# Channel attention and two feed-forward layers on one core: the float64 weights' low word added as an integer on VectorE

## The chip, the cores and the metric

One core of a Trainium2 chip. The time is device microseconds (us) of one launch; loading inputs and storing the output are in it. Engines: TensorE (PE, with its weight loads as PEld), VectorE (DVE), ScalarE (ACT), GpSimd (POOL) and SyncE (SP), which issues all DMAs here.

## What is computed

q, k and v are [6016, 256], float32. The attention runs over channels, and its output goes through two layers with 2048 hidden columns.

```python
qn = q / (np.linalg.norm(q, axis=1, keepdims=True) + 1e-06)
kn = k / (np.linalg.norm(k, axis=1, keepdims=True) + 1e-06)
s = kn.transpose(0, 2, 1) @ qn / tau
a = softmax(s)                           # 256 x 256
x = v @ a                                # 6016 x 256
h = x @ moe_w_in;  g = h - np.tanh(h);  x = g @ moe_w_out
h = x @ moe2_w_in; g = np.where(h > 0, h, np.exp(np.minimum(h, 0)) - 1)
return g @ moe2_w_out
```

The four weights (256 x 2048 or 2048 x 256) are float64: each is two 32-bit words, low and high.

## The kernel before

Every float32 operand of a product is held as two float32r parts, hi and lo, and a product is hi·hi + hi·lo + lo·hi: three matmuls.

**Attention, up to about 56 us.** q and k come in chunks; their squared norms and the 256 x 256 scores are summed, then the softmax is taken and transposed. The first conversions of weights already run there.

**Folding.** The softmax's matrix is multiplied into the first layer's w_in in place (`fold_attention`, in eight parts: "aw", twelve matmuls of 128x256 each, L406), so that v itself enters the first layer. `evac_fold` writes hi on ScalarE (L428) and lo on VectorE (L434).

**The two layers.** Tokens go in 13 blocks of up to 464, columns of the hidden layer in eight pairs of 128. A unit is (layer, block, pair) and is one step of the last loop. In each step TensorE's order is: the unit's h (`emit_h`, twelve matmuls of 128x464, L406), a fold where one is due, and o of the unit two steps before (`emit_out`, twelve matmuls, L574). h lies in one of two PSUM buffers. It is free once VectorE has read it: in layer 0 by g = h - tanh(h) (L494), in layer 1 by L517. A fold from the third on uses one of these two buffers as well. All instructions stand in an order written out by hand; each engine takes its own in that order.

The first ten steps alternate between blocks 0 and 1 of layer 0, six more finish them, eight do block 2, and then units of layer 1 and layer 0 come in turn.

**The conversion of the weights** (`class Converter`) is what the change touches. A unit of it is 512 elements on each partition (24 early units) or 256 (16 late ones), and it goes through stages one step apart, put between the instructions of `emit_act`:

- `load`: the two words by DMA, into one of 4 (late: 3) buffers;
- `first`, ScalarE: the high word's square (L104, "sq") and the low word scaled (L105, "low");
- `second`, VectorE, four instructions that `fill(0)` to `fill(3)` place in the step: flushed (L121), which zeroes what float32 can't hold; shifted (L127) and joined (L133), which build float32's bits of the value cut to 20 bits of mantissa ("cut"); and power (L139), which leaves its power of two in "hz";
- `third_scalar`, ScalarE, in the next step: hi, rounded by its type (L159), from "cut";
- `third_pool`, GpSimd, in the next step: low · power (L167), cut - hi (L168), and their sum, lo (L169).

VectorE's order in a step of blocks 0 to 2 is flushed, L494, L434 where a part was folded, shifted, joined, lo of g (L522), power. ScalarE's is tanh (L493), L428 where a part was folded, hi of the unit before, sq and low of the next, hi of g (L505). L522 waits for L505. From block 3 on, and in layer 1, VectorE rounds g's hi itself (L503, L521). "hz" and "cut" have two buffers each, "sq" two (late: one), "low" four (late: three).

Once the early units are through, their memory is given to the second layer's w_out, and the late units' loads begin. One core does all of it.

Of the kernel before, what the change touches and what calls it, by code (L numbers as in the profile page):

```python
# [8 lines left out]
F32 = mybir.dt.float32  # L9
F32R = mybir.dt.float32r  # L10
U32 = mybir.dt.uint32
AF = mybir.ActivationFunctionType
# [4 lines left out]
P = 128  # L17
#: The high word of 2^-126 as a float64, read as a float32: smaller weights are float32 zeros.
TINY_HIGH = 2.0**-15 * 1.125
# [3 lines left out]
def kernel(  # L23
# [11 lines left out]
):  # L35
    """q, k: [N, C]; vT: [C, N]; the weights: float64 words as [.., .., 2] (low, high); outT: [C, N].

    A float32 operand of a product is held as two parts of 12 significant bits, hi + lo, both
    float32r, so that hi*hi + hi*lo + lo*hi is float32's product to its last bit.
    """  # L40
    nc = tc.nc
# [19 lines left out]

# [1 line left out]
    # A unit is (layer, which, first column or row of d_ff, their number): 2 words of d_ff x C  # L63
    # for each of them on a partition. It goes through its stages one tick apart, so that no
    # engine waits for another within a tick.

    class Converter:
# [29 lines left out]
        def first(self):  # L97
            """ScalarE: the high word's square and the low word's value below 2^-20."""
            if self.at[1] == self.at[0]:
                return  # L100
            s = self.st[self.at[1]]
            s["sq"] = self.tmp.tile([P, self.n], F32, tag="sq", name="sq", bufs=self.nsq)
            s["low"] = self.tmp.tile([P, self.n], F32, tag="low", name="low", bufs=self.nlow)
            nc.scalar.activation(out=s["sq"], in_=s["raw"][:, :, 1].bitcast(F32), func=AF.Square)  # L104
            nc.scalar.activation(out=s["low"], in_=s["raw"][:, :, 0], func=AF.Copy, scale=2.0**-52)  # L105
            self.at[1] += 1

        def second(self):
            """VectorE: float32's bits of the value cut to 20 of the mantissa, and of its power of 2."""
            if self.begun == self.at[1]:  # L110
                return []
            s = self.st[self.begun]
            self.begun += 1
            hz = self.tmp.tile([P, self.n], F32, tag="hz", name="hz")
            cut = self.tmp.tile([P, self.n], U32, tag="cut", name="cut")
            s["pow"], s["cut"] = hz, cut.bitcast(F32)
            high = hz.bitcast(U32)

            def flushed():
                # Zero where the float64 is below float32's normal range.  # L120
                nc.vector.scalar_tensor_tensor(  # L121
                    out=hz, in0=s["sq"], scalar=TINY_HIGH**2, in1=s["raw"][:, :, 1].bitcast(F32),
                    op0=ALU.is_ge, op1=ALU.mult,
                )

            def shifted():
                nc.vector.tensor_scalar(  # L127
                    out=cut, in0=high, scalar1=3, scalar2=0x3FFFFFF8,
                    op0=ALU.logical_shift_left, op1=ALU.bitwise_and,
                )  # L130

            def joined():
                nc.vector.scalar_tensor_tensor(  # L133
                    out=cut, in0=high, scalar=0xC0000000, in1=cut,
                    op0=ALU.bitwise_and, op1=ALU.bitwise_or,
                )

            def power():
                nc.vector.tensor_scalar(  # L139
                    out=high, in0=cut, scalar1=0xFF800000, scalar2=None, op0=ALU.bitwise_and  # L140
                )
                self.at[2] += 1

            return [flushed, shifted, joined, power]

# [6 lines left out]
        def third_scalar(self):  # L152
            """ScalarE: hi, rounded by its type."""
            if self.at[3] == self.at[2]:
# [6 lines left out]
        def third_pool(self):  # L161
            """GpSimd: lo = (cut - hi) + low * power of 2."""
            if self.at[3] == self.at[2]:
                return
            s = self.st.pop(self.at[3])
            low, cut = self.shape(s["low"]), self.shape(s["cut"])
            nc.gpsimd.tensor_tensor(out=low, in0=low, in1=self.shape(s["pow"]), op=ALU.mult)  # L167
            nc.gpsimd.tensor_tensor(out=cut, in0=cut, in1=s["hi"].bitcast(F32), op=ALU.subtract)  # L168
            nc.gpsimd.tensor_tensor(out=s["lo"], in0=cut, in1=low, op=ALU.add)  # L169
            self.at[3] += 1  # L170

    NU = KC * 2 * P
    # w_in is wanted a step ahead of its phase's h, w_out two steps after it.
    SIDE = NP - 3
# [11 lines left out]
    aT_pool = right.enter_context(tc.tile_pool(name="aT", bufs=1, side="right"))  # L186
    # The scores' transpose: for each half of k's channels, q's on the partitions.
    aT_hi = [aT_pool.tile([P, KC, P], F32R, name=f"aT_hi{m}") for m in range(KC)]
    aT_lo = [aT_pool.tile([P, KC, P], F32R, name=f"aT_lo{m}") for m in range(KC)]
    rsum = aT_pool.tile([P, KC], F32, name="rsum")  # L190

# [1 line left out]
    v_of = {}  # L193
# [20 lines left out]
    def attention():  # L214
        with ExitStack() as init:
# [8 lines left out]
            nc.vector.memset(tiny, 1e-36)  # L224
            # The table for the squares and the root is fetched while the first loads are on their way.
            nc.scalar.activation(out=root[:, 0:1], in_=tiny, func=AF.Sqrt)
# [11 lines left out]
            chunks = [(j, min(J, JT - j)) for j in range(0, JT, J)]  # L238
            # Every other chunk's product goes in parts: PE would be behind the loads.
            in_parts = [i % 2 == 1 and i < len(chunks) - 2 for i in range(len(chunks))]  # L240
# [18 lines left out]
            def keep_warm(n):  # L259
                """PE's clock falls when it has nothing to do."""  # L260
                for _ in range(n):
# [48 lines left out]
            for part_of in early.second():  # L310
                part_of()
            # One column of squared norms for each half of q's and of k's channels.
            for t in range(2):
# [22 lines left out]
            keep_warm(3)  # L336
            # 1 / |q| along the free axis, the same on every partition.
            rq = ps_q.tile([P, KC, 512], F32, tag="sq", name="rq", bufs=2)[:, 0, :C]
# [10 lines left out]
            sm = one.tile([P, KC], F32, name="sm")  # L349
            # a: the negative of the scores. Of the softmax, the division by the sum comes with  # L350
            # the product with w_in.
            nc.vector.tensor_scalar_mul(a[:, 0, :], S[0], rk[:, 0:1])
# [32 lines left out]
    with tc.manual_schedule():  # L385
# [16 lines left out]
        def product(out, terms):  # L402
            """out = the sum over terms of lhsT.T @ rhs, each of which is (hi, lo); w_lo comes last."""
            pairs = [(w[0], x) for w, xs in terms for x in xs] + [(w[1], xs[0]) for w, xs in terms]
# [3 lines left out]
        def fold_attention(p):  # L408
            """w_in of the first layer, in place: softmax(..) @ w_in, for v in x's place."""
            fs = slice(2 * P * p, 2 * P * (p + 1))  # L410
# [11 lines left out]
        def evac_fold(p, ps):  # L422
            """With the softmax's division; the parts of it for the two engines."""
            fs = slice(2 * P * p, 2 * P * (p + 1))
# [37 lines left out]
        def emit_act(layer, b, p, h, ticks, fold):  # L462
# [10 lines left out]
            def between():  # L473
                """ScalarE's and GpSimd's part of the conversion."""
                if ticks == 1:
# [5 lines left out]
            if ticks == 2:  # L481
                thirds()
            # VectorE's, each step of which waits for the one before, goes between the others.
            seconds = [conv.second() for _ in range(ticks)]
# [21 lines left out]
            else:  # L506
                # exp(m) - 1 = tanh(m / 2) * (exp(m) + 1), m = min(h, 0): no cancellation near 0.
                e = (late_pool[0] if late_pool else spool_e).tile([P, 2, width], F32, tag="e", name="e")[:, :, :n]
# [17 lines left out]
        def emit_last_act(b, p, h):  # L526
            """The last unit's, one tile of d_ff after the other and on more engines: nothing hides it."""
            _, n = blocks[b]
# [34 lines left out]
        def emit_out(layer, b, p, g):  # L563
# [4 lines left out]
            hi, lo = g  # L568
            # g's lower part comes last.
            for w, x in ((wout_hi, hi), (wout_lo, hi), (wout_hi, lo)):  # L570
# [31 lines left out]
        def interleaved(first, second, lead):  # L602
            """The units of two phases in turn; the second starts `lead` units later."""
            first = [(*first, p) for p in range(NP)]
# [8 lines left out]

        # A phase starts once the output of the one that it reads is on its way.
        order = [(0, b, p) for p in range(SIDE) for b in range(2)]
# [93 lines left out]
```

## Time and profile before

| | |
|---|---|
| time, median of 3 runs | 1149.56 us (1149.43 to 1152.14) |
| span of the profiled execution (its first to its last instruction; the page has no other time of it) | 1147.9 us |
| PE busy | 1116.2 us, 97%, 5360 instructions |
| PEld busy | 991.2 us, 86% |
| DVE busy | 879.0 us, 77%, 957 instructions |
| ACT busy | 555.5 us, 48% |
| POOL busy | 178.3 us, 16%, 137 instructions |
| mean granted TensorE clock | 0.996 |

The page cuts the span into 40 equal slices (28.7 us each); a digit is the busy share in tenths:

```profile
PE   8889998999999999999999999999999999999998
DVE  6999998899866767766677777676776667678776
POOL 5577676355100000000000000000000000000000
```

In the rows below, times are us from the span's start. A busy time of pipelined instructions overlaps the next one's a little; where an argument needs what an instruction costs its engine, it goes from start to start.

### The profile page before, as it was taken

Reading aid. Unit: us, or ns where it says so; the run is one execution under the profiler, and the core shown is the slowest. Engines: PE = TensorE matmul, PEld = TensorE weight load, DVE = VectorE, ACT = ScalarE, POOL = GpSimd, SP = SyncE. Lnnn points to the kernel's source line nnn. Section 1 sums busy time; section 2 is a strip of 40 time slices with the busy share of each in tenths; the row PEclk is TensorE's granted clock in tenths of the full one; section 3 lists DMA queues with packets and bytes.
Section 4 is the critical chain, followed back from the end, with each engine's and each line's share of the span. In section 5 each row is a group of like instructions: output and inputs, shape, how many; then the busy total and the mean of one; then the engine's idle time right before and its main releaser. Section 6 shows DMA issues by size and latency. Waiting matters only on the chain.

```text
span 1147.9 us, 13713 instructions
## 1 busy us (share of the span) xinstructions
PE 1116.2 (97%) x5360; PEld 991.2 (86%) x5360; DVE 879.0 (77%) x957; ACT 555.5 (48%) x662; POOL 178.3 (16%) x137
## 2 busy tenths in 40 slices
PE   8889998999999999999999999999999999999998
PEld 7778887787888888888888888888888889998897
DVE  6999998899866767766677777676776667678776
ACT  7766664664444443444444334434334444445664
POOL 5577676355100000000000000000000000000000
PEclk9999998999999999999999999999999999999999
DMA  9632220220100100100001001001001000000000
GB/s 349 225 109 77 90 90 1 74 67 24 34 1 1 34 1 1 34 1 29 5 1 34 1 1 34 1 1 34 1 1 33 1 12 5 1 17 1 1 34 17
DMA packets 23040, 42.30 MB, mean 37 GB/s; under 512 B 1984, under 2 KB 8896, under 8 KB 22976
## 3 DMA queue, kind: packets, MB, share of 16 engines
q1 hardware_dynamic: 22976, 41.43, 10.8%
q8 instruction: 42, 0.69, 0.2%
q14 instruction: 22, 0.18, 0.0%
HBM read 35.26 MB, written 6.16 MB: 36 GB/s over the span
## 4 chain that ended last, share of the span: by engine, by line
PE 82%; DVE 7%; issue 7%; ACT 1%; POOL 1%; DMA 1%; SPq 0%; DVEq 0%; ACTq 0%
PE h L406 40%; PE o L574 39%; PE S L249 3%; DVE hz L121 1%; DVE cut L127 1%; DVE hz L139 1%; DVE g L517 1%; DVE cut L133 1%; DVE g L494 1%; DMA qk<-in_k_dram 1%; POOL cut L168 0%; POOL win_lo L169 0%; PE aw L406 0%; DVE glo L522 0%; DVE win_lo L434 0%
## 5 line engine op out<-in xcount | busy, mean ns | idle before, releaser
L513 DVE SCALAR_TENSOR_TENSOR g<-e,g 128x928 f32<-128x928 f32 (+1 forms) x103 | 118.9, 1155 | 194.3 <-ACT e L511 194.3
L522 DVE TENSOR_TENSOR glo<-g,ghi 128x928 fp32r<-128x928 f32 (+1 forms) x207 | 242.9, 1173 | 22.4 <-ACT ghi L505 2.7
L509 ACT ACTIVATE e<-h 128x928 f32<-128x928 f32 (+1 forms) x103 | 97.3, 945 | 312.8 <-PE h L406 312.8
L574 PE MATMUL o<-ghi,wout_lo 128*128 128x464 f32 (+1 forms) x832 | 208.7, 372 | 1.6 <-POOL wout_lo L169 1.6
L574 PE MATMUL o<-ghi,wout_hi 128*128 128x464 f32 (+1 forms) x832 | 209.2, 373 | 0.4 <-DVE xlo L591 0.3
L574 PE MATMUL o<-glo,wout_hi 128*128 128x464 f32 (+1 forms) x832 | 208.7, 372 | 0.0
L493 ACT ACTIVATE g<-h 128x928 f32<-128x928 f32 (+1 forms) x104 | 98.0, 942 | 157.6 <-PE h L406 157.6
L574 PEld LDWEIGHTS o<-ghi,wout_lo 128*128 128x128 f32 x832 | 156.1, 188 | 20.6 <-POOL wout_lo L169 2.4
L574 PEld LDWEIGHTS o<-glo,wout_hi 128*128 128x128 f32 x832 | 156.0, 188 | 19.0 <-DVE glo L522 0.2
L574 PEld LDWEIGHTS o<-ghi,wout_hi 128*128 128x128 f32 x832 | 156.4, 189 | 18.5 <-PE h L406 0.7
L406 PE MATMUL h<-vhi,win_hi 128*128 128x464 f32 (+1 forms) x416 | 156.2, 375 | 9.3 <-DVE g L494 8.6
L406 PE MATMUL h<-xhi,win_hi 128*128 128x464 f32 (+1 forms) x414 | 154.6, 374 | 5.6 <-DVE g L517 4.4
L406 PE MATMUL h<-vlo,win_hi 128*128 128x464 f32 (+1 forms) x416 | 155.9, 375 | 0.0
L406 PE MATMUL h<-xlo,win_hi 128*128 128x464 f32 (+1 forms) x414 | 153.5, 371 | 0.0
L517 DVE SCALAR_TENSOR_TENSOR g<-h,g 128x928 f32<-128x928 f32 (+1 forms) x103 | 115.5, 1122 | 10.0
L406 PE MATMUL h<-vhi,win_lo 128*128 128x464 f32 (+1 forms) x416 | 121.5, 373 | 0.3 <-DVE win_lo L434 0.3
L406 PE MATMUL h<-xhi,win_lo 128*128 128x464 f32 (+1 forms) x414 | 119.9, 370 | 0.0
L494 DVE TENSOR_TENSOR g<-h,g 128x928 f32<-128x928 f32 (+1 forms) x104 | 115.8, 1114 | 0.7 <-ACT g L493 0.7
L510 ACT ACTIVATE g<-e 128x928 f32<-128x928 f32 (+1 forms) x103 | 101.0, 981 | 3.2
L511 ACT ACTIVATE e<-e 128x928 f32<-128x928 f32 (+1 forms) x103 | 100.8, 978 | 3.3
L406 PEld LDWEIGHTS h<-vhi,win_hi 128*128 128x128 f32 x416 | 78.5, 189 | 22.3 <-DVE g L494 7.4
L406 PEld LDWEIGHTS h<-xhi,win_hi 128*128 128x128 f32 x414 | 77.7, 188 | 17.4 <-DVE g L517 7.2
(113 smaller groups left out, 1149.2 us busy)
## 6 DMA issues: line engine op xcount, KB each, us to landing
qk<-in_q_dram SPq DMA_DIRECT2D x23, 256.0 KB, 5.1
qk<-in_k_dram SPq DMA_DIRECT2D x23, 256.0 KB, 5.2
vraw<-in_vT_dram SPq DMA_DIRECT2D x12, 464.0 KB, 4.4
out_dram<-osb SPq DMA_DIRECT2D x12, 464.0 KB, 2.9
raw0in<-in_moe_w_in_dram SPq DMA_DIRECT2D x8, 512.0 KB, 3.8
raw0out<-in_moe_w_out_dram SPq DMA_DIRECT2D x8, 512.0 KB, 3.7
raw1in<-in_moe_w_in_dram SPq DMA_DIRECT2D x8, 512.0 KB, 3.8
raw1out<-in_moe_w_out_dram SPq DMA_DIRECT2D x16, 256.0 KB, 2.6
```

Source lines behind the costliest of these rows:

```text
L121: nc.vector.scalar_tensor_tensor(out=hz, in0=s["sq"], scalar=TINY_HIGH**2, in1=s["raw"][:, :, 1].bitcast(F32), op0=ALU.is_ge, op1=ALU.mult,)
L249: nc.tensor.matmul(out=S[m], lhsT=kk[:, 1, j, m * P : (m + 1) * P], rhs=qq[:, 0, j, :], start=(count[m] == 1), stop=(count[m] == total),)
L406: nc.tensor.matmul(out=out, lhsT=w, rhs=x, start=(i == 0), stop=(i == len(pairs) - 1))
L493: nc.scalar.activation(out=g, in_=h, func=AF.Tanh)
L494: nc.vector.tensor_tensor(out=g, in0=h, in1=g, op=ALU.subtract)
L509: nc.scalar.activation(out=e, in_=h, func=AF.Relu, scale=-1.0)
L510: nc.scalar.activation(out=g, in_=e, func=AF.Tanh, scale=-0.5)
L511: nc.scalar.activation(out=e, in_=e, func=AF.Exp, scale=-1.0)
L513: nc.vector.scalar_tensor_tensor(out=g, in0=e, scalar=1.0, in1=g, op0=ALU.add, op1=ALU.mult)
L517: nc.vector.scalar_tensor_tensor(out=g, in0=h, scalar=0.0, in1=g, op0=ALU.max, op1=ALU.add)
L522: nc.vector.tensor_tensor(out=lo, in0=g, in1=hi.bitcast(F32), op=ALU.subtract)
L574: nc.tensor.matmul(out=o[:, c, :n], lhsT=w[layer][:, f, c * P : (c + 1) * P], rhs=x[:, i], start=(f == 0 and w is wout_hi and x is hi), st ...
```

## The change

The low word is scaled by 2^-29 instead of 2^-52 and written as uint32, so that it becomes an integer of three bits, rounded. VectorE's fourth instruction is now the add of this integer to the bits of "cut", where it was the power of two's mask. GpSimd's part is one subtraction, cut - hi, into lo. Comments and docstrings are taken out as well; line numbers stay.

```diff
-            s["low"] = self.tmp.tile([P, self.n], F32, tag="low", name="low", bufs=self.nlow)
+            s["low"] = self.tmp.tile([P, self.n], U32, tag="low", name="low", bufs=self.nlow)
             nc.scalar.activation(out=s["sq"], in_=s["raw"][:, :, 1].bitcast(F32), func=AF.Square)
-            nc.scalar.activation(out=s["low"], in_=s["raw"][:, :, 0], func=AF.Copy, scale=2.0**-52)
+            nc.scalar.activation(out=s["low"], in_=s["raw"][:, :, 0], func=AF.Copy, scale=2.0**-29)
...
-            s["pow"], s["cut"] = hz, cut.bitcast(F32)
+            s["cut"] = cut.bitcast(F32)
...
-            def power():
-                nc.vector.tensor_scalar(
-                    out=high, in0=cut, scalar1=0xFF800000, scalar2=None, op0=ALU.bitwise_and
-                )
+            def rounded():
+
+                nc.vector.tensor_tensor(out=cut, in0=cut, in1=s["low"], op=ALU.add)
                 self.at[2] += 1
 
-            return [flushed, shifted, joined, power]
+            return [flushed, shifted, joined, rounded]
...
             s = self.st.pop(self.at[3])
-            low, cut = self.shape(s["low"]), self.shape(s["cut"])
-            nc.gpsimd.tensor_tensor(out=low, in0=low, in1=self.shape(s["pow"]), op=ALU.mult)
-            nc.gpsimd.tensor_tensor(out=cut, in0=cut, in1=s["hi"].bitcast(F32), op=ALU.subtract)
-            nc.gpsimd.tensor_tensor(out=s["lo"], in0=cut, in1=low, op=ALU.add)
+            nc.gpsimd.tensor_tensor(
+                out=s["lo"], in0=self.shape(s["cut"]), in1=s["hi"].bitcast(F32), op=ALU.subtract
+            )
             self.at[3] += 1
```

## Rows read from the trace of the kernel before

**Rows 1.** Stretches: length, busy us of each engine (instructions), clock, DMA share, GB/s.

```profile
56.57:87.50 30.93, 26.13 (x121) 22.01 (x122) 30.69 (x37) 20.59 (x33) 22.11 (x15) 0.94 0.32 101
87.50:138.12 50.62, 48.15 (x254) 42.85 (x253) 50.34 (x60) 32.57 (x51) 35.77 (x25) 1.00 0.28 84
138.12:205.54 67.42, 59.47 (x265) 50.72 (x263) 60.74 (x62) 36.49 (x52) 45.12 (x30) 0.95 0.19 61
205.54:298.50 92.96, 88.19 (x409) 76.18 (x410) 88.39 (x124) 52.38 (x84) 43.51 (x48) 1.00 0.13 40
```

**Rows 2.** The chain that ended last: start, us, what.

```profile
122.81 1.42 PE aw L406 x12
124.23 2.52 PE o L574 x12
126.74 2.53 PE h L406 x12
```

**Rows 3.** TensorE's waits, 56 to 299 us: us in total, times, longest.

```profile
PE h L406 <- DVE g L494: 9.7, 9, 3.9
PE h L406 <- DVE g L517: 4.4, 7, 1.9
PE aw L406 <- DVE g L494: 3.4, 1, 3.4
PE o L574 <- POOL wout_lo L169: 1.6, 2, 0.9
```

**Rows 4.** VectorE's timeline, two steps around 100 us: start, us, instruction.

```profile
93.68 1.11 DVE L494 TENSOR_TENSOR g<-h,g 128x928 f32<-128x928 f32 x1
94.71 0.86 DVE L434 SCALAR_TENSOR_TENSOR win_lo<-aw,rsum,win_hi 128x256 fp32r<-128x256 f32 x2
...
99.42 0.68 DVE L121 SCALAR_TENSOR_TENSOR hz<-sq,raw0in 128x512 f32<-128x512 f32 x1
100.02 1.11 DVE L494 TENSOR_TENSOR g<-h,g 128x928 f32<-128x928 f32 x1
101.06 0.48 DVE L127 TENSOR_SCALAR cut<-hz 128x512 uint32<-128x512 uint32 x1
101.57 1.68 DVE L133 SCALAR_TENSOR_TENSOR cut<-hz,cut 128x512 uint32<-128x512 uint32 x1
103.17 2.21 DVE L522 TENSOR_TENSOR glo<-g,ghi 128x928 fp32r<-128x928 f32 x1
105.30 0.41 DVE L139 TENSOR_SCALAR hz<-cut 128x512 uint32<-128x512 uint32 x1
...
106.24 1.11 DVE L494 TENSOR_TENSOR g<-h,g 128x928 f32<-128x928 f32 x1
```

**Rows 5.** GpSimd's timeline in the same step; the bracket is its idle time before.

```profile
99.58 1.67 POOL L167 TENSOR_TENSOR low<-low,hz 128x512 f32<-128x512 f32 x1 [2.00 <-DVE hz L139]
101.21 1.48 POOL L168 TENSOR_TENSOR cut<-cut,wout_hi 128x512 f32<-128x512 f32 x1
102.77 1.62 POOL L169 TENSOR_TENSOR wout_lo<-cut,low 128x512 fp32r<-128x512 f32 x1
```

**Rows 6.** VectorE's timeline in the attention.

```profile
40.58 0.69 DVE L299 TENSOR_TENSOR acc<-acc 128x512 f32<-128x512 f32 x1
```

**Rows 7.** ScalarE's timeline, the next step.

```profile
104.23 0.84 ACT L428 ACTIVATE win_hi<-aw,rsum 128x256 fp32r<-128x256 f32 x2 [0.47 <-PE aw L406]
104.96 0.63 ACT L159 ACTIVATE win_hi<-cut 128x512 fp32r<-128x512 f32 x1
105.48 0.68 ACT L104 ACTIVATE sq<-raw0out 128x512 f32<-128x512 f32 x1
...
107.44 0.98 ACT L505 ACTIVATE ghi<-g 128x928 fp32r<-128x928 f32 x1 [0.72 <-DVE g L494]
```

**Rows 8.** VectorE's groups, 205 to 292 us: busy us, mean ns, idle before.

```profile
L513 DVE SCALAR_TENSOR_TENSOR g<-e,g 128x928 f32<-128x928 f32 x8 | 12.2, 1527 | 1.0 <-ACT e L511 1.0
L133 DVE SCALAR_TENSOR_TENSOR cut<-hz,cut 128x256 uint32<-128x256 uint32 x16 | 10.6, 662 | 0.3
```

## The prediction

> **What bounds the kernel now.** I read the page's busy row and its forty slices first: TensorE is busy 97% of the span, so only the stretches where it is not can be won. Behind about 299 us its slices are full until the last; there every cut on VectorE or GpSimd is hidden. The conversion runs from 40 to 294 us, and the loss lies there, from the first h at 56.57 us on.
>
> How much it is follows from counting. One group of twelve matmuls (an h or an o) takes 2.525 us when nothing holds it, one fold (aw) 1.42 [rows 2]. The count of matmuls in each stretch is that of its groups: A, 56.57 to 87.50, holds 5 h, 3 o and 2 folds (23.0 us of work in 30.93: 7.9 lost); B, to 138.12, 8 h, 8 o, 5 folds (47.5 in 50.62: 3.1 lost); C, to 205.54, 11 h and 11 o (55.6 in 67.42: 11.9 lost); D, to 298.50, 17 h and 17 o (85.9 in 92.96: 7.1 lost) [rows 1]. Together 30.0 us: idle time, the refilling after each stop, and a granted clock that averages 0.94 and 0.95 in A and C, where TensorE had stood for its longest waits, 3.4 and 3.9 us [rows 1, 3].
>
> What it waits for is nearly always VectorE's subtraction that frees an h buffer (L494, L517), twice GpSimd's wout_lo [rows 3]. VectorE's line shows why: two steps of the loop, from one L494 to the next, take 6.34 and 6.22 us without a gap, while TensorE needs 6.47 with a fold and 5.05 without, 11.5 for the two [rows 2, 4]. VectorE is the bound in these stretches, and it is slower than its own work. Start to start, L494 takes 1.04 and the subtraction L522 of the same size 2.13; L121 takes 0.60 and L133, with as many elements and two inputs too, 1.60 [rows 4]. The long ones stand beside GpSimd: L168 runs from 101.21 to 102.69 and L133, begun at 101.57, ends 0.56 later; L169 ends at 104.39 and L522 1.0 later [rows 4, 5]. They do their work only once GpSimd's operation is over. L494, which reads one operand from PSUM, runs at full pace beside L167.
>
> The Trainium skill's page "SBUF — State Buffer", section "Who interferes with whom", says that VectorE and GpSimd share a port pair as an exclusive lock: an instruction of VectorE with two SBUF inputs, or in a two-port mode, waits for all of a GpSimd operation that reads SBUF, or makes it wait. These rows agree.
>
> **The change, part by part.** *GpSimd* loses two of three operations a unit, L167 and L169 or L168 (about 1.5 us each with their waits) [rows 5]. GpSimd is no bound itself; what counts is that VectorE is held by one operation a unit, not by two.
>
> *VectorE.* L139 (0.33 start to start) goes, an add of two uint32 tiles comes [rows 4]. The trace has no integer add. Nearest is the float32 add of the same size, 0.69 long, 0.61 start to start less the overlap of 0.08 that its neighbours show [rows 4, 6]; below, it can cost no less than L139's 0.33; above, no more than a two-input uint32 operation that is held, L133's 1.60. I take 0.61, since L133 shows that type alone doesn't slow it: once free, it needs 0.56. So 0.28 more a unit.
>
> A step without a fold was 0.60 + 1.04 + 0.51 + 1.60 + 2.13 + 0.33 = 6.21. Without any hold it becomes 0.60 (L121) + 1.04 (L494) + 0.42 (L127, at L139's length) + 0.60 (L133) + 1.04 (L522) + 0.61 (add) = 4.31; a step with a fold has 0.79 more for L434, 5.10. To it comes the hold of the one operation that is left, 0 to 1.25 (one operation's own time: L169 ends 1.22 after 103.17, where L133 has made way [rows 4, 5]). Where does it fall? GpSimd now starts when ScalarE's hi (L159) is done, and hi waits for the add, the last VectorE step of the unit. With VectorE behind, hi ends about 0.6 after the add; GpSimd then runs from 0.65 to 1.9 after it. VectorE does L121 until 0.60 and L494 until 1.64: only 0.26 of L127 is held, and nothing in a fold step, where L434 covers it too. I take 4.57 and 5.10. Two steps: 9.7 beside TensorE's 11.5 in B; 4.57 beside 5.05 in C. TensorE becomes the bound in both.
>
> *ScalarE.* The low word's activation keeps its size, and I cost its changed scale and type at nothing: ScalarE works 32.6 of B's 50.6 us [rows 1], and what it took longer would first use up the 0.3 us named below. hi now waits for the add instead of L133: a new wait at the head of an in-order queue. Behind it stand sq and low of the next unit and ghi, for which L522 waits. From the add's end: 0.55 + 0.57 + 0.57 + 0.88 = 2.6 until ghi [rows 7], while VectorE has 0.60 + 1.04 + 0.26 + 0.42 + 0.60 = 2.9 to do before L522. So it is covered, by 0.3.
>
> *By stretch.* A: the start is serial. L494 of the first h comes about 1.7 earlier (fewer holds ahead of it); the first fold step stays near 6.2, since GpSimd there falls just on L127; the next takes 4.55. The second fold's wait shrinks from 3.4 to about 2, the next h waits 0.6, refills make it 2.9 lost instead of 7.9: gain 5.0, the slow clock included. B: all 3.1. C: VectorE also splits v, twice subtracts x's high part (1.04 each) and does two units in one step (2.1 and perhaps a hold); these five us and more pile up over six steps that win 0.48 each, against 5.4 us that L494 may be late before an h waits (7.6 from an h's end to the h that reuses its buffer, less 2.1 for the tanh and L494). About 1.4 stays lost: gain 10.5. The wout_lo waits go, since the one operation follows hi at once. D has units of half the size; L513 there averages 1.53 where its like takes 1.11, L133 0.66 [rows 8]. A pair of steps took 92.96 / 8.5 = 10.9 against TensorE's 10.1; the four holds that I count in it (L133, L127, L513 and L127 again) come to near 2 and one short one stays, so that the pair falls to about 9.5. I leave 0.7 lost for the steps that also split v or x: gain 6.4.
>
> Sum: 5.0 + 3.1 + 10.5 + 6.4 = 25.0. The page gives the profiled execution's span alone, 1147.9; the median of the runs, 1149.56, lies 1.66 above it, which I take as what surrounds it. 1147.9 − 25.0 + 1.66 = **1124.5 us**. Behind 299 us nothing hides or returns the gain, as TensorE has no gap there.
>
> **Rivals.** *One operation still holds VectorE for its whole length* (17%). For it: the hold in the first fold step, and the two held instructions in each step now [rows 4, 5]. Then the steps are 5.56 and 6.35: A gains 3.5, B 0.35 a step or 2.8, C 0.65 × 8 and 1.1 at the hand-over of the pools, 6.3 in all, D next to nothing: 12.6, 1137. Against it: hi's place right ahead of L494. By the Trainium skill's rule alone, without asking what is beside the operation, the sum would be this one.
>
> *No change* (5%): the add takes 1.60 or more each time and the single hold falls elsewhere in the same step: 4.31 + 1.0 + 1.25 = 6.56 without a fold, where it was 6.21, and 7.35 with one; the cheaper start, GpSimd's earlier wout_lo and smaller late units give about as much back: 1148 to 1151. Against it: one operation can hold one instruction only once.
>
> *Slower* (4%): hi's new wait. If the hold falls on L522 or the add, and the tanh, which stands ahead of hi in ScalarE's queue, falls into the ring too, then hi, sq, low, ghi, L522, the add and the tanh make 2.6 + 1.04 + 0.61 + 1.25 + 0.88 (L505's size) = 6.38, and 7.1 with L428 [rows 7], against 6.22 and 6.34. It decides once a ring passes 6.3, and over some 22 units with 8 folds costs 0.16 × 14 + 0.77 × 8 = 8: 1157. Against it: the tanh follows ghi at once and has L522 and the add, 1.65 us, to hide beside.
>
> **How the numbers follow.** My forecast, TensorE bound nearly everywhere, has 74%; within it the gain runs from 18 to the 30.0 that there are (1119.6 to 1131.6). The range goes from 1119 to 1137, the first rival's middle; half of that rival and the two others, near 2 in 10, lie outside. Both signs: faster 0.91 (forecast and first rival), within 0.3% (3.4 us, about what a measurement here can tell from none) 0.05, slower 0.04.
>
> **What would show it.** Right: about a quarter fewer VectorE us between 60 and 200 us; L522 near 1.1 and L133 near 0.7 on the mean; the add near 0.69; PE's waits for L494 and L517 in single us; no slow clock near 180 us; GpSimd's busy time from 178 to near 80. Wrong step by step: an add of over 1 us (its price); L127 or L522 still held each step (the place of the hold); ScalarE's waits for the add followed by L522 waiting for ghi (the ring); a stop of over 3 us in A (the start). The prediction fails if VectorE still shows no gap between 130 and 200 us and TensorE waits there as before.

## The result and the profile after

The changed kernel takes 1122.83 us (median of 4 runs, 1122.68 to 1123.31) beside 1149.55 for the kernel before on the same chip: a ratio of 0.9761, with a 95% interval of 0.9747 to 0.9774. The forecast was 1124.5. The spans of the two profiled executions go from 1147.9 to 1121.3 us.

The page of the changed kernel, busy time of the engines:

```profile
PE 1109.8 (99%) x5360; PEld 992.0 (88%) x5360; DVE 851.1 (76%) x957; ACT 554.9 (49%) x662; POOL 75.0 (7%) x57
```

TensorE has the same 5360 matmuls and now works 99% of the span. GpSimd went from 178.3 to 75.0 us. VectorE has the same 957 instructions and lost 28 us.

The four stretches again, from the same h to the same h (columns as in [rows 1]):

```profile
55.32:82.30 26.98, 25.18 (x121) 22.15 (x121) 25.69 (x38) 20.31 (x33) 7.20 (x6) 0.94 0.39 117
82.30:129.65 47.35, 47.35 (x254) 43.00 (x253) 46.02 (x59) 31.82 (x51) 10.42 (x9) 1.00 0.29 89
129.65:185.76 56.11, 55.71 (x265) 49.40 (x264) 50.82 (x63) 37.66 (x54) 12.92 (x10) 1.00 0.23 74
185.76:271.81 86.05, 86.00 (x409) 76.50 (x408) 80.29 (x122) 51.64 (x83) 16.00 (x16) 1.00 0.15 43
```

The matmuls are as many as in [rows 1], so the lengths compare directly: A 30.93 to 26.98, B 50.62 to 47.35, C 67.42 to 56.11, D 92.96 to 86.05. That is 3.95 + 3.27 + 11.31 + 6.91 = 25.4, and the first h starts 1.25 earlier: 26.7, which is the whole difference of the spans (26.6) to rounding. Against the work counted in the prediction (23.0, 47.5, 55.6, 85.9), the loss is now 4.0, 0, 0.5 and 0.2: nearly all that is left lies in A.

Line numbers behind the conversion have moved: L494 of the kernel before is L492 here, L522 is L520, L434 is L432, and lines that an experiment adds shift them again (L495, L523). TensorE's waits from 52 to 299 us (us in total, times, longest), the lines that answer to [rows 3]:

```profile
PE aw L404 <- DVE g L492: 1.8, 1, 1.8
...
PE h L404 <- DVE g L492: 0.4, 1, 0.4
```

Nine waits of h for the subtraction (L494 before, L492 now) have become one of 0.4. Those for L517 and for GpSimd's wout_lo are gone. Left out are two at the start, of 0.7 and 0.6 us, which are the same in both kernels.

VectorE's groups from 60 to 205 us (times, busy us, mean ns, idle before):

```profile
L520 DVE TENSOR_TENSOR glo<-g,ghi 128x928 fp32r<-128x928 f32 x26 | 29.1, 1121 | 3.6 <-ACT ghi L503 3.1
L127 DVE TENSOR_SCALAR cut<-hz 128x512 uint32<-128x512 uint32 x21 | 19.1, 911 | 0.1
L133 DVE SCALAR_TENSOR_TENSOR cut<-hz,cut 128x512 uint32<-128x512 uint32 x21 | 14.4, 691 | 0.7
L140 DVE CUSTOM_DVE_ANT_0 cut<-cut,low 128x1024 uint16<-128x1024 uint16 x21 | 14.3, 685 | 0.0
```

The same groups in the same window of the kernel before:

```profile
L522 DVE TENSOR_TENSOR glo<-g,ghi 128x928 fp32r<-128x928 f32 x22 | 34.8, 1582 | 2.2 <-ACT ghi L505 2.2
L133 DVE SCALAR_TENSOR_TENSOR cut<-hz,cut 128x512 uint32<-128x512 uint32 x22 | 32.7, 1490 | 0.7
L127 DVE TENSOR_SCALAR cut<-hz 128x512 uint32<-128x512 uint32 x22 | 15.6, 713 | 0.2
```

The first two now run as long as their elements need. L127 is longer than before: in most steps the one hold that is left falls on it. In a run below that takes the hold away it has 0.42; with that as its free length the holds on these three came to 10.1 + 17.6 + 6.4 = 34 us before (22 of each) and come to 0.49 × 21 = 10 now. The add (L140, under the name that the trace gives it, as 16-bit halves) takes 0.685 us where the mask took 0.465.

VectorE's and GpSimd's timelines around 100 us (start, us, instruction, idle before), which answer to [rows 4, 5]:

```profile
98.86 0.88 DVE L432 SCALAR_TENSOR_TENSOR win_lo<-aw,rsum,win_hi 128x256 fp32r<-128x256 f32 x2 [0.18 <-ACT win_hi L426]
99.65 1.36 DVE L127 TENSOR_SCALAR cut<-hz 128x512 uint32<-128x512 uint32 x1
101.05 0.69 DVE L133 SCALAR_TENSOR_TENSOR cut<-hz,cut 128x512 uint32<-128x512 uint32 x1
101.65 1.12 DVE L520 TENSOR_TENSOR glo<-g,ghi 128x928 fp32r<-128x928 f32 x1
102.69 0.69 DVE L140 CUSTOM_DVE_ANT_0 cut<-cut,low 128x1024 uint16<-128x1024 uint16 x1
103.29 0.69 DVE L121 SCALAR_TENSOR_TENSOR hz<-sq,raw0out 128x512 f32<-128x512 f32 x1
104.02 1.12 DVE L492 TENSOR_TENSOR g<-h,g 128x928 f32<-128x928 f32 x1
105.06 1.10 DVE L127 TENSOR_SCALAR cut<-hz 128x512 uint32<-128x512 uint32 x1
```

```profile
99.42 1.30 POOL L165 TENSOR_TENSOR win_lo<-cut,win_hi 128x512 fp32r<-128x512 f32 x1 [5.05 <-ACT win_hi L158]
104.58 1.30 POOL L165 TENSOR_TENSOR win_lo<-cut,win_hi 128x512 fp32r<-128x512 f32 x1 [3.85 <-ACT win_hi L158]
```

GpSimd's L165 ends at 100.72 and L127, begun at 99.65, ends 0.29 later; the next ends at 105.88 and L127 0.28 later. L492 and L432, which read PSUM, stand beside the same operation at full pace. In these steps all of L133, L520, L140 and L121 is free of it. In C, where a step also splits v or x or does two units, the hold falls on L121 instead (1.80 us at 138.86, 1.62 at 145.56, free 0.69); the eight L121 of the second layer's w_in average 1060 ns, 3 us above their free length in all, where they averaged 1157 before.

### The profile page after: what moved, and what is told of

Its sections match the earlier page's. It is cut to its first block, busy times and chain, and to the rows that moved or that the text cites. A ratio compares the mean times of both kernels' runs of the same rounds, so it can differ in the third digit from the quotient of the medians.

```text
span 1121.3 us, 13606 instructions
## 1 busy us (share of the span) xinstructions
PE 1109.8 (99%) x5360; PEld 992.0 (88%) x5360; DVE 851.1 (76%) x957; ACT 554.9 (49%) x662; POOL 75.0 (7%) x57
## 4 chain that ended last, share of the span: by engine, by line
PE 89%; DVE 6%; issue 2%; ACT 2%; DMA 1%; SPq 0%; POOL 0%; ACTq 0%; DVEq 0%; POOLq 0%
PE h L404 42%; PE o L572 42%; PE S L247 3%; DVE glo L520 1%; PE aw L404 1%; DVE hz L121 1%; DVE cut L140 1%; DVE cut L127 1%; DMA qk<-in_k_dram 1%; DVE g L492 0%; ACT ghi L503 0%; DVE cut L133 0%; DVE g L515 0%; DVE xlo L589 0%; ACT g L491 0%
## 5 line engine op out<-in xcount | busy, mean ns | idle before, releaser
L511 DVE SCALAR_TENSOR_TENSOR g<-e,g 128x928 f32<-128x928 f32 (+1 forms) x103 | 116.8, 1134 | 197.2 <-ACT e L509 197.2
L520 DVE TENSOR_TENSOR glo<-g,ghi 128x928 fp32r<-128x928 f32 (+1 forms) x207 | 232.4, 1123 | 22.8 <-ACT ghi L503 3.1
L492 DVE TENSOR_TENSOR g<-h,g 128x928 f32<-128x928 f32 (+1 forms) x104 | 116.1, 1116 | 1.6 <-ACT g L491 1.4
L404 PEld LDWEIGHTS h<-vlo,win_hi 128*128 128x128 f32 x416 | 78.1, 188 | 9.6
```

The source lines that it names most:

```text
L404: nc.tensor.matmul(out=out, lhsT=w, rhs=x, start=(i == 0), stop=(i == len(pairs) - 1))
L492: nc.vector.tensor_tensor(out=g, in0=h, in1=g, op=ALU.subtract)
L511: nc.vector.scalar_tensor_tensor(out=g, in0=e, scalar=1.0, in1=g, op0=ALU.add, op1=ALU.mult)
L520: nc.vector.tensor_tensor(out=lo, in0=g, in1=hi.bitcast(F32), op=ALU.subtract)
```

## The experiments

All edits are made to the changed kernel; ratios are to the kernel before, which took 1149.55 to 1150.09 us on the four chips, so that times of different chips compare to about half a us. "Behind the subtraction" means GpSimd's L165.

**Is it GpSimd's time beside VectorE, or the shorter way to lo?** Two operations that nobody reads are put behind the subtraction. lo comes as early as in the changed kernel, but VectorE has three operations beside it again.

```diff
+            spare = s["low"].bitcast(F32)
+            for _ in range(2):
+                nc.gpsimd.tensor_tensor(out=spare, in0=spare, in1=spare, op=ALU.mult)
```

> Two further GpSimd operations a unit, of the size of the one that is left, behind it, on a tile that nothing waits for soon; lo is ready as early as in the changed kernel, and its value is the same. Theory 1, the hold: GpSimd's operations that read SBUF keep VectorE's two-input and two-port instructions waiting for their whole length. Three in a step again: 4.31 us of VectorE work, the add included, plus about 2.3 held makes 6.5 without a fold and near 7 with one: 1147 to 1158 us, with L133 or L520 at 1.6 and 2.1 us again. Rival, the shorter chain: the gain came from GpSimd's lo being ready two operations earlier (wout_lo, win_lo, and the buffers that it frees): 1122 to 1125.

Measured: 1153.14 us, ratio 1.0027 (1.0017 to 1.0038). VectorE's groups from 60 to 205 us, then TensorE's waits from 52 to 299:

```profile
L523 DVE TENSOR_TENSOR glo<-g,ghi 128x928 fp32r<-128x928 f32 x22 | 34.1, 1552 | 2.2 <-ACT ghi L506 2.2
L133 DVE SCALAR_TENSOR_TENSOR cut<-hz,cut 128x512 uint32<-128x512 uint32 x22 | 29.5, 1344 | 0.7
```

```profile
PE h L407 <- DVE g L495: 12.4, 8, 4.3
...
PE aw L407 <- DVE g L495: 3.4, 1, 3.4
```

The whole gain is gone, and both the long instructions and the waits of [rows 3] are back, though no matmul waits for a low part. (Three more waits of h, 2.5 us, are put down to ScalarE's L105; no matmul reads its output, and each of them ends 0.15 us after an L495.) So the gain is the time that VectorE is held. That lo comes earlier is worth nothing that this shows. The 0.27% above the kernel before may be the add that is longer than the mask; no run tests it.

**How does it grow?** The same with one operation.

```diff
+            spare = s["low"].bitcast(F32)
+            for _ in range(1):
+                nc.gpsimd.tensor_tensor(out=spare, in0=spare, in1=spare, op=ALU.mult)
```

> One further GpSimd operation a unit instead of two. Theory 1, the hold: a step without a fold takes 4.31 + 0.26 + about 1.0 = 5.5 against TensorE's 5.05, with a fold 6.3 against 6.47, so that VectorE is the bound again in the first steps and from 130 to 180 us only: 1130 to 1140 us. Rival, the shorter chain: 1122 to 1125, as with two more.

Measured: 1134.41 us, ratio 0.987 (0.9853 to 0.9886). VectorE's groups from 60 to 205 us:

```profile
L523 DVE TENSOR_TENSOR glo<-g,ghi 128x928 fp32r<-128x928 f32 x25 | 28.0, 1121 | 3.2 <-ACT ghi L506 2.8
L133 DVE SCALAR_TENSOR_TENSOR cut<-hz,cut 128x512 uint32<-128x512 uint32 x21 | 25.2, 1204 | 0.7
```

None, one and two more operations give 1122.8, 1134.4 and 1153.1. The first further one costs 11.6 us and falls on L133; the second costs 18.7 and falls on the subtraction of glo. The first costs nothing in B, which takes 47.35 us (84.27 to 131.62) as in the changed kernel: there VectorE had slack for it. C and D take 61.62 and 89.78 instead of 56.11 and 86.05.

**What does a GpSimd operation hold that reads nothing?** Two fills in the same place; they write the same tile.

```diff
+            spare = s["low"].bitcast(F32)
+            for _ in range(2):
+                nc.gpsimd.memset(spare, 0.0)
```

> Behind the subtraction GpSimd fills the spent tile of the low word with zeros, twice a unit: two operations that write SBUF and read nothing, in place of the two that read. The hold by reads (the Trainium skill, SBUF - State Buffer, Who interferes with whom: two SBUF inputs contend with a GpSimd operation that reads SBUF, not with one that only writes): L133 and L520, with two inputs, stay at 0.7 and 1.1 us; only L127, the one of a single input, can be held: 1123 to 1130. Rival, any GpSimd operation holds them: as with two more that read, scaled to the fill's own length, 1135 to 1153.

Measured: 1129.64 us, ratio 0.9824 (0.9809 to 0.9838). Groups of VectorE and GpSimd from 60 to 205 us:

```profile
L127 DVE TENSOR_SCALAR cut<-hz 128x512 uint32<-128x512 uint32 x21 | 23.9, 1140 | 0.1
L133 DVE SCALAR_TENSOR_TENSOR cut<-hz,cut 128x512 uint32<-128x512 uint32 x21 | 14.4, 692 | 0.7
L170 POOL MEMSET low<- 128x512 f32 x44 | 26.0, 591 | 1.3
```

L133, with two inputs, is as free as without the fills (692 ns beside 691); L127, with one input, is held longer (1140 beside 911). One step shows it, first with the two fills and then with the one further operation of the run before:

```profile
96.62 0.69 DVE L133 SCALAR_TENSOR_TENSOR cut<-hz,cut 128x512 uint32<-128x512 uint32 x1
...
95.78 1.26 POOL L170 MEMSET low<- 128x512 f32 x2
```

```profile
96.93 1.41 DVE L133 SCALAR_TENSOR_TENSOR cut<-hz,cut 128x512 uint32<-128x512 uint32 x1
...
96.56 1.23 POOL L170 TENSOR_TENSOR low<-low 128x512 f32<-128x512 f32 x1
```

The second fill, which ends at 97.04, leaves L133 its 0.69; the operation that reads makes it 1.41. So it is no general slowing by a busy GpSimd: which instruction waits depends on what both read and write. The subtraction of glo shows nothing here: it starts at 97.23, after the fills. The Trainium skill's page "SBUF — State Buffer", section "Who interferes with whom", has a two-input instruction of VectorE contend with a GpSimd instruction that reads SBUF and not with one that only writes it, while two-port modes contend with either. L133's rows agree with the first; L127's fit the second if it runs in such a mode, which no row names (it needs 0.42 us for as many elements as take L133 0.69).

**What does the add cost?** The mask stands in its place again (the low words are left out of the sum). ScalarE's hi then waits for L133 and no longer for the fourth instruction; what that alone is worth is the run on hi's new wait, below.

```diff
-                nc.vector.tensor_tensor(out=cut, in0=cut, in1=s["low"], op=ALU.add)
+                nc.vector.tensor_scalar(
+                    out=high, in0=cut, scalar1=0xFF800000, scalar2=None, op0=ALU.bitwise_and
+                )
```

> VectorE's fourth instruction is the old mask of the power of two (into hz) in place of the add, so the low words are left out of the weights; GpSimd keeps its one subtraction. Theory 1: the add costs 0.28 us a unit more than the mask, and VectorE is not the bound behind 77 us, so only the three steps at the start come earlier, 0.8 us, and with them perhaps the slow clock behind the second fold's wait, 1.7: 1120 to 1123. Rival, VectorE is still the bound: 0.28 x 24 + 0.13 x 16 = 9 less: about 1114.

Measured: 1121.85 us, ratio 0.9754 (0.974 to 0.9769). The longer add, some 0.2 us a unit, costs 1.0 us in the whole kernel: most of it is hidden. The second fold's stop and the stretch behind it (windows as above):

```profile
PE aw L406 <- DVE g L494: 1.4, 1, 1.4
```

```profile
67.98:76.43 8.45, 7.01 (x37) 5.80 (x37) 8.38 (x13) 7.70 (x13) 2.88 (x2) 1.00 0.64 182
```

The stop is 1.4 instead of 1.8 and no slow clock follows. The 1.0 us lies in A, which takes 26.03 here (first h 55.52, sixth 81.55) instead of 26.98.

**How much of the time that VectorE won is spare?** A second add, into a tile that nobody reads.

```diff
                 nc.vector.tensor_tensor(out=cut, in0=cut, in1=s["low"], op=ALU.add)
+                nc.vector.tensor_tensor(out=high, in0=cut, in1=s["low"], op=ALU.add)
```

> VectorE adds twice: the second add's result, in hz, is read by nothing, so the weights are those of the changed kernel; hi and lo wait for the first add as before. Theory 1: VectorE has slack behind the start: a step without a fold is 4.31 + 0.61 + 0.26 = 5.2 against TensorE's 5.05, with a fold 5.8 against 6.47. Lost are 3 x 0.6 in the first steps, a fall of the clock there, and up to 3 us of the nine steps from 130 to 180 us with their extra work: 1125 to 1129. Rival, VectorE is still the bound through the whole conversion: 0.61 x 24 + 0.34 x 16 = 20: 1143. Rival, it has slack everywhere: 1123.

Measured: 1138.58 us, ratio 0.9899 (0.9882 to 0.9915): far above what was expected. The four stretches:

```profile
55.79:86.18 30.39, 27.01 (x121) 23.37 (x121) 29.08 (x42) 20.46 (x33) 7.14 (x6) 0.89 0.35 102
86.18:133.52 47.34, 47.34 (x253) 42.98 (x252) 46.79 (x67) 32.20 (x51) 10.50 (x9) 1.00 0.30 90
133.52:194.75 61.23, 57.89 (x266) 50.28 (x264) 55.95 (x71) 36.73 (x52) 14.75 (x10) 0.97 0.22 67
194.75:287.05 92.30, 87.95 (x410) 76.01 (x409) 87.45 (x140) 52.91 (x84) 15.01 (x16) 1.00 0.14 41
```

Against the changed kernel's stretches, A is 3.4 longer, B the same, C 5.1 and D 6.2. B has slack for the 0.69; C and D have hardly any. In D a pair of VectorE's steps takes 9.75 us in the changed kernel (its L511 starts at 212.94 and at 222.69) beside TensorE's 10.08: 0.3 to spare, where a second add of two half units takes 0.7. A's loss has a slow clock in it (0.89). The edit also moves the hold: L127's mean falls from 911 to 608 ns, and the second add averages 780 where the first has 684.

**Does hi's new wait cost anything?** The add goes into the other tile, hi is taken from cut ahead of it as in the kernel before, and GpSimd subtracts from the sum.

```diff
-            s["cut"] = cut.bitcast(F32)
+            s["cut"], s["sum"] = cut.bitcast(F32), hz
...
-                nc.vector.tensor_tensor(out=cut, in0=cut, in1=s["low"], op=ALU.add)
+                nc.vector.tensor_tensor(out=high, in0=cut, in1=s["low"], op=ALU.add)
...
-                out=s["lo"], in0=self.shape(s["cut"]), in1=s["hi"].bitcast(F32), op=ALU.subtract
+                out=s["lo"], in0=self.shape(s["sum"]), in1=s["hi"].bitcast(F32), op=ALU.subtract
```

> The add writes into hz, and hi is rounded from the bits before the add (lo = sum - hi is then exact all the same): ScalarE no longer waits for the add. Theory 1: the new wait is covered (2.6 us of ScalarE beside 2.9 of VectorE), so it costs nothing: 1122 to 1123.5. Rival, the new wait costs: up to the 35 us that ScalarE stands before hi come off its queue, and where ghi or exp comes late through it TensorE gains up to 2 us: 1120 to 1121.5. Against both: GpSimd's operation may fall on another instruction, 0.5 us either way.

Measured: 1123.0 us, ratio 0.9766 (0.9751 to 0.978), the same as the changed kernel. ScalarE's waits from 40 to 300 us, in the changed kernel and then in this one:

```profile
ACT wout_hi L158 <- DVE cut L140: 25.1, 12, 3.7
ACT win_hi L158 <- DVE cut L140: 8.2, 7, 1.6
```

```profile
ACT wout_hi L158 <- DVE cut L133: 7.8, 7, 1.6
ACT sq L104 <- DVE hz L121: 17.4, 14, 2.0
```

The wait for the add is real, 33 us in all, and costs nothing that these times show: taken away, ScalarE waits as well at the next conversion (sq). The edit has a price of its own, 0.6 us in which TensorE waits for the first win_lo (L432), so that a few tenths of a gain could be hidden. A takes 26.48 here, with its clock at 1.00; B, C and D are within 0.1 of their lengths in the changed kernel. VectorE's wait for ghi is the same in both, 3.1 us in four times between 60 and 205 us.

**Can the rest in A be had?** In a fold step hi's call comes ahead of the fold's own evacuations, so that GpSimd's subtraction stands beside L492 and L432, which read PSUM.

```diff
-                if ticks == 1:
+                if ticks == 1 and not fold:
                     thirds()
...
                 if fold:
+                    if ticks == 1:
+                        thirds()
                     scalar, vector = evac_fold(*fold)
```

> In a step with a fold, ScalarE's hi of the weights and with it GpSimd's subtraction come ahead of L426 (the fold's win_hi) instead of behind it. Theory 1: GpSimd then runs beside L492 and L432, which read PSUM, and L127 is held no more in these steps (1.3 us becomes 0.45). In the first step that comes 0.87 earlier on VectorE's path to the second fold, whose wait of 1.8 us becomes about 0.9; in the other fold steps it changes no time, TensorE being the bound: 1120 to 1122, the lower end if the clock does not fall behind that wait. Rival, the wait in the first steps is set by ScalarE's or TensorE's order and not by the hold: 1122.8, or some 0.3 more as L426 comes later.

Measured: 1122.02 us (1121.69 to 1122.28), ratio 0.9755 (0.9741 to 0.977). The first fold step, in the changed kernel and then in this one (VectorE's and GpSimd's timeline):

```profile
61.61 1.29 DVE L127 TENSOR_SCALAR cut<-hz 128x512 uint32<-128x512 uint32 x1
...
61.32 1.30 POOL L165 TENSOR_TENSOR wout_lo<-cut,wout_hi 128x512 fp32r<-128x512 f32 x1 [4.70 <-ACT wout_hi L158]
```

```profile
61.42 0.42 DVE L127 TENSOR_SCALAR cut<-hz 128x512 uint32<-128x512 uint32 x1
...
59.80 1.30 POOL L165 TENSOR_TENSOR wout_lo<-cut,wout_hi 128x512 fp32r<-128x512 f32 x1 [3.37 <-ACT wout_hi L158]
```

The same operation of GpSimd, 1.5 us earlier, holds nothing: L127 is 0.42 instead of 1.29. L432 takes 0.88 us in both, from 60.82 and from 60.62. The second fold's stop falls from 1.8 to 1.0, with no slow clock behind it, and A takes 25.44 (first h 55.13, sixth 80.57) instead of 26.98. With the clock up, the next h waits 0.6 us instead (75.44). This version and the changed kernel again, on another chip beside the same kernel before:

> hi ahead of L426 in the fold steps, once more. Theory 1: 0.8 to 1.5 us below the changed kernel on the same chip, by the shorter hold in the first step and the clock that does not fall: 1121.5 to 1122.3. Rival, the difference seen before was between chips: the same time as the changed kernel beside it.

> The changed kernel once more, beside the next on the same chip: 1122.5 to 1123.5 us. If the clock falls behind the second fold's wait of 1.8 us again, that fall belongs to the kernel and not to one execution.

The moved call gave 1122.16 (1121.60 to 1122.52), ratio 0.9755 (0.9742 to 0.9769), the changed kernel 1123.0 (1122.66 to 1123.93), ratio 0.9763 (0.9749 to 0.9776). Both times the moved call is 0.8 us lower and the two ranges of runs don't overlap; the intervals of the ratios do. In the second profiles A takes 26.96 and 25.43, as in the first. That the times differ by 0.8 and the profiles' A by 1.5 fits a slow clock that not every execution of the changed kernel has: its nine runs have mean granted clocks of 0.998 to 1.000, the moved call's eight all 1.000. Of the versions that keep the low words it is probably the best, by 0.07%.

**Both together** (the edit of hi from cut, whose lines of the add and of the subtraction are as above, and the moved call):

```diff
-            s["cut"] = cut.bitcast(F32)
+            s["cut"], s["sum"] = cut.bitcast(F32), hz
...
-                if ticks == 1:
+                if ticks == 1 and not fold:
                     thirds()
...
                 if fold:
+                    if ticks == 1:
+                        thirds()
```

> hi ahead of L426 in the fold steps, and hi from the bits before the add. Theory 1: as with hi ahead of L426 alone, 1121.5 to 1122.3, since the second edit frees only what is covered; in the second and third step it may save some 0.2 of L127's hold of 0.35. Rival, the new wait costs in the first steps: near 1121.

Measured: 1122.11 us (1121.98 to 1122.95), ratio 0.9759 (0.9745 to 0.9774): not below the moved call alone.

## Why the prediction was right

**The bound and the hold: right.** TensorE waited for VectorE, and VectorE for GpSimd. Putting GpSimd's time back restores the waits and the time; putting back two fills, which leave L133 free, costs 6.8 us, where two operations that read cost 30 and one that is as long as both fills (1.25 us) costs 11.6. The rival by which one operation still holds its whole length (1137) falls by its time: even two operations a unit gave 1134.4. Its premise was nearer: in B the one operation holds L127 for 0.7 to 0.9 us of its 1.30.

**The add's price: right.** 0.685 us against 0.69, 0.60 from start to start against 0.61, and its bounds were not needed. With it no change at 1148 to 1151 falls.

**hi's new wait: right.** It exists and is covered; the slower rival falls by the run without it (1123.0).

**The place of the hold that is left: half right.** I said that 0.26 us of L127 is held in a step without a fold and nothing in one with. Where VectorE sets the pace it is near that: L127 takes 0.75 to 0.78 at the start, so 0.35, and the steps there are 4.69 and 4.67 long where 4.57 was said (from L492 at 65.78 to 70.47 to 75.14). But in B, once TensorE sets the pace, L127 takes 1.10 and in fold steps 1.36, and the reason given for the fold step, that L434 covers it, fails: ScalarE's hi stands behind the fold's evacuations in its queue, so that GpSimd starts only at L432's middle. L127 still held in each step was one of the prediction's signs of a wrong step, and here it is one. It cost nothing in B, which has the slack, and A's first fold step paid for it.

**By stretch.** B 3.27 for 3.1, C 11.3 for 10.5, D 6.9 for 6.4. A is the mis-sized one, 3.95 for 5.0. Its stops came as forecast, 1.8 and 0.4 for "about 2" and 0.6. The clock did not:

```profile
67.18:77.24 10.06, 8.26 (x37) 7.26 (x36) 9.99 (x15) 8.02 (x13) 2.70 (x3) 0.83 0.50 160
72.00:75.00 3.00, 3.00 (x15) 2.89 (x14) 2.97 (x5) 2.18 (x4) 0.00 (x0) 0.52 0.88 326
```

The second of these windows of the changed kernel shows TensorE busy without a gap at a granted clock of 0.52, near the lower of its two levels (1.2 of 2.4 GHz), behind the stop of 1.8. I had counted the slow clock of A as gone with the longer stop. With the moved call, the stretch of the same matmuls has it at 1.00:

```profile
66.98:75.44 8.46, 6.85 (x37) 5.65 (x36) 8.43 (x12) 6.05 (x10) 2.32 (x2) 1.00 0.49 169
```

1.6 us less for 37 matmuls. The stop is 0.8 shorter; TensorE is busy for 1.4 less at the full clock, and 0.6 of that goes to the wait of the next h, so that the clock is worth about 0.8 as well.

**Not foreseen: 1.25 us ahead of the first h.** I looked at the holds from 56 us on. In the attention VectorE has an instruction of 128x2 elements that stood beside L169 before (L345, 1.10 us from 48.68, GpSimd's operation from 48.48 to 49.76) and now takes

```profile
48.31 0.23 DVE L343 TENSOR_SCALAR rk<-quot,itau 128x2 f32<-128x2 f32 x1
```

0.87 us for an instruction of a few elements. The other 0.4 is there already at 41.8 us, when the data come, but the second profile of the changed kernel, on another chip, does not have it: there the first h starts at 55.76, 0.8 earlier than before, and L343 takes 0.23 again. So the 0.4 is not the change's. This 1.25 makes up for the 1.05 that A lacks, the 0.4 of it by luck; the 1.7 by which the forecast was too high is mostly C's 0.8 and D's 0.5.

**The margin: wrong, and without cost here.** I put D's pair at 9.5 beside 10.1 and let C keep 1.4 of loss. The pair takes 9.75, and the second add shows that C and D were at their edge: the second add there (0.69 a unit, 0.42 for D's half units) cost 5.1 and 6.2 us. C lost only 0.5, less than I left for its six full steps, but with next to nothing to spare.

**Of the signs,** one was wrong in size: "a quarter fewer VectorE us". The busy time of A to C falls from 141.8 to 122.5, by 14%. The holds' 34 us became 10 and the add took 4 more, some 20 us; the quarter was right only for a step without a fold that splits a unit, and many steps have more in them than that.

## What to carry to other kernels

GpSimd's cost on a kernel is not its busy share (16% here) but which of VectorE's instructions it stands beside: compare the same instruction's duration with and without a GpSimd operation beside it, and price each operation by that. Where the operation must stay, put it beside VectorE's instructions that read PSUM; the moved call made one hold of 0.87 us vanish for nothing. And a gain that ends when another engine takes over says nothing on the slack behind it: doubling one cheap instruction (the add, 0.69 us) measures it by stretch, if what it shifts on the other engines is read with it.

## What the hardware showed that I had not expected

The clock fell behind a stop of 1.8 us in the changed kernel and again in its second profile (0.60 from 72 to 75 us), and stayed at 1.00 behind second-fold stops of 1.52 (hi from cut), 1.4 (the mask) and 1.0 (the moved call, both times). That looks like a matter of the stop's length, but the other runs don't bear it out. It fell behind stops of 2.3 with the second add (0.56 from 75 to 78 us) and 2.4 with the fills (0.72 from 72 to 75), but with one further GpSimd operation it stayed up behind a longer stop, which ends at 73.67:

```profile
PE aw L407 <- DVE g L495: 2.6, 1, 2.6
```

```profile
72.00:78.00 6.00, 4.22 (x24) 3.59 (x24) 5.97 (x8) 4.88 (x9) 2.45 (x2) 1.00 0.50 167
```

So the stop's length alone does not decide it. What else does was not tried.

A small instruction is held like a large one: L345, with 128x2 elements, lost 0.87 us to one GpSimd operation, and in the runs with one and two further operations it takes 0.75 where one of them stands beside it, 0.23 without. A count of elements would have left it out.
